# Linear attention and RWKV channel mixing in one kernel: weight halves, new instruction orders and filler matmuls at the start

## Chip, cores and metric

The kernel runs on one core of a Trainium2 chip. The metric is the device time of one execution in microseconds (us); the median of several runs counts. Engines are PE (TensorE), DVE (VectorE), ACT (ScalarE), POOL (GpSimd) and SP (SyncE). PE's matrix results go to PSUM banks, from which DVE or ACT copies them on.

## What is computed

```python
# q, k, v: (8 batches, 8 heads, 576 rows, 64), float32
q_s = softmax(q, axis=-1)                       # over the 64 features of a row
k_s = softmax(k, axis=2)                        # over the 576 rows
kv  = einsum('bhsd,bhse->bhde', k_s, v)
x   = einsum('bhsd,bhde->bhse', q_s, kv)        # heads side by side: (8, 576, 512)

x_prev = x shifted down by one row, first row zero
xk = mu_k * x + (1 - mu_k) * x_prev
xr = mu_r * x + (1 - mu_r) * x_prev
k  = relu(xk @ w_k)                             # (512 x 1024)
v  = (k * k) @ w_v                              # (1024 x 512)
out = sigmoid(xr @ w_r) * v                     # w_r (512 x 512); out (8, 576, 512)
```

## The kernel before

**Attention.** Work comes in units (b, g): batch b and half g of its heads, four heads in two pairs. For each unit ACT takes the exponential of q and k (`exp`) and casts v (`cast_v`), DVE sums q's exponentials (`rsum`), inverts (`rrec`) and scales (`scale_q`, into tiles `qs`). PE transposes the scaled q (`transpose_q`, L498, 36 small matmuls of 64x64 against an identity) and forms kv (`kv`, L475, 36 small matmuls); a column of ones in v's tiles gives the sums for k's softmax. ACT or DVE copies the transposed q to `qt`. For batches 0 and 1 (`ON_PE`) the mixing with `x_prev` is done on PE: DVE makes weights `wp` from kv, its reciprocal sums `rz` and the mu values (`weights_of`, L555), one set for xk and one for xr, and PE multiplies them with `qt` (`by_heads`, L511) for each half h of the 576 rows; ACT or DVE then copies the result into `xk` or `xr` (`copy_mixed`, L568). For the later batches PE only forms x, and DVE does the mixing (L613 to L627).

**Channel mixing.** The rows of four batches lie in a ring of 2304 columns, cut into units of 512, 512, 512, 512 and 256 columns, twice. For each unit PE makes the eight chunks fc of `xk @ w_k` (`k_part`, L712, four matmuls for each chunk over the contraction tiles ct), ACT takes the relu (L697), DVE squares it into `k_a` or `k_b` (L701). Then for every 128 rows PE does `xr @ w_r` (`r_part`, L745), ACT the tanh that makes the sigmoid (L750), PE `k*k @ w_v` in two halves of four matmuls (`v_part`, L755), DVE the gating (L761), and SP stores the rows (L772). In the first two units the chunks are done four at a time, contraction tiles 0 and 1 of all four first (they need only g = 0 and the first half of w_k, `wk0`), then tiles 2 and 3 (g = 1 and `wk1`). These are called the first and the second pairs below; each pair is two matmuls.

**Loads.** The six loads of batch 0 are issued by ACT and SP, in two halves each. All others are issued by POOL and turn float32 weights into bfloat16 on the way; the first of them waits until load number `GATE` of batch 0 has landed. `LOADS` gives their order up to batch 1: `wk0` and `wk1` for w_k, `wv0` and `wv1`, `wr`, `mu`, and names like `q10b` for q of batch 1, group 0, second half. A unit's loads go to buffers `raw_a` to `raw_l`.

**Order.** Nothing is scheduled by hand. Each operation is added to a `Plan` with its engine, an assumed time on the engine and until its result, a key (a due time) and the operations that it depends on. `Plan.order` walks through an assumed time line: on each engine it takes, of the operations that can start within `LOOK` of the earliest, the one that is due first, and it hands out the PSUM slots (`mm_a` to `mm_d`, two `att` slots of two banks) as they come free. The operations are then issued in the order of these starts; the engines run them in that order. Constants of the model (`SPARE`, `LOOK`, `EARLY`, `MAIN`, `PACE`, the DMA terms) therefore decide the order of instructions on every engine, and the chip decides when they run. `ALONE` decides for which units of the later batches the x matmuls are issued alone instead of together with the next unit's transposes.

`filler` emits matmuls of the identity with itself into a free `mm` slot. They have the latest due time, so the planner takes one only when PE has nothing else, and drops those that would start after `FILL_END`:

```python
            if op.due >= 1.5 * LATE and t > FILL_END:
                continue
```

In the kernel before, `FILL` is 0, so there are none.

Of the kernel before, what the change touches and what calls it, by code (L numbers as in the profile page):

```python
# [8 lines left out]
ACT = mybir.ActivationFunctionType  # L9
# [7 lines left out]
START = 0.7  # L17
HOP = 0.05
LATE = 1e6
SPARE = 0.142  # L20
LOOK = {"PE": 0.017, "ACT": 0.686, "DVE": 0.274, "POOL": 0.03, "SP": 0.03}
EARLY = (-0.88, 2.53, 7.27, 7.81, 6.48, 1.05, 4.91, 4.86, 2.31, 3.67, 7.48, 5.23, -5.83,
         4.63, 1.92, 1.86)
EARLY_R = -0.92
MAIN = 17.0
PACE = 1.05
DMA_RATE = 404.0
DMA_LEAD = 1.75
DMA_TAIL = 0.55
# [2 lines left out]
FIRST = ((0, 0, ("ACT", "ACT")), (0, 1, ("SP", "SP")), (0, 2, ("SP", "SP")),  # L32
         (1, 0, ("SP", "SP")), (1, 1, ("SP", "SP")), (1, 2, ("SP", "SP")))
ORDER = (0, 1, 2)
LOADS = ("wk0", "q10b", "wk1", "v10a", "q10a", "wr", "k10a", "wv0", "mu", "v10b", "k10b",
         "wv1", "k11b", "q11b", "q11a", "k11a", "v11a", "v11b")
GATE = 7
FILL = 0
FILL_AT = 1
FILL_END = 15.0  # L40
ON_PE = (0, 1)
CASTS = (("POOL", "POOL"), ("ACT", "DVE"), ("ACT", "ACT"))
QCOPY = ("ACT", "ACT", "DVE")
WIDE = "ACT"
ALONE = 8
EVAC = ((("ACT", "DVE"), ("ACT", "DVE")), (("DVE", "ACT"), ("ACT", "ACT")))


# [23 lines left out]
class Plan:  # L72
# [60 lines left out]
    def order(self):  # L133
        self.set_due()
        free = {}
        self.pe_busy = []
        dma_free = 0.0
        tiled = False
        missing, since = {}, {}
        open_ops = {}  # L140
        for op in self.ops:
            missing[op] = len(op.deps)
            since[op] = 0.0
            open_ops.setdefault(op.engine, [])
            if not op.deps:
                open_ops[op.engine].append(op)
        done = []
        left = len(self.ops)
        while left:
            chosen = None  # L150
            for engine, ops in open_ops.items():
                now = free.get(engine, START)
                ready = None
                for op in ops:
                    t = max(now, since[op])
                    if ready is not None and max(t, now + LOOK[engine]) > ready[0][0]:
                        continue
                    but = []
                    for slot in op.takes:
                        got = self.slot_time(slot, but)  # L160
                        if got is None:
                            break
                        but.append((slot.pool, got[1]))
                        t = max(t, got[0] + HOP)
                    if len(but) < len(op.takes):
                        continue
                    rank = (max(t, now + LOOK[engine]), op.due)
                    if ready is None or rank < ready[0]:
                        ready = (rank, t, op)
                if ready is not None and (chosen is None or ready[1] < chosen[1]):  # L170
                    chosen = ready
            assert chosen is not None, "no operation can start"
            _, t, op = chosen
            open_ops[op.engine].remove(op)
            left -= 1
            if op.due >= 1.5 * LATE and t > FILL_END:
                continue
            for slot in op.takes:
                slot.index = self.slot_time(slot)[1]
                for part in self.pools[slot.pool][slot.index]:  # L180
                    self.user[part] = slot
            occ, lat = op.occ, op.lat
            if op.engine == "PE":
                if not self.warm(t):
                    occ, lat = op.cold * occ, lat + (op.cold - 1) * occ
                if op.tiled != tiled:
                    tiled = op.tiled
                    occ, lat = occ + 0.1, lat + 0.1
                self.pe_busy.append((t, t + occ))
            op.start, op.end = t, t + lat  # L190
            if op.size and op.size < 20:
                op.end += 2.2 if op.key < 0 else 6.0
            elif op.size:
                dma_free = max(dma_free, t + DMA_LEAD) + op.size / DMA_RATE
                op.end = dma_free + DMA_TAIL
                if op.engine == "POOL":
                    op.end += 1.4 if op.size > 1000 else 0.6
            free[op.engine] = t + occ
            for o in self.after.get(op, ()):
                missing[o] -= 1  # L200
                since[o] = max(since[o], op.end + HOP)
                if not missing[o]:
                    open_ops[o.engine].append(o)
            done.append(op)
        return sorted(done, key=lambda o: o.start)
# [3 lines left out]
def kernel(  # L209
# [12 lines left out]
    nc = tc.nc  # L222

    B, H, S, D = q.shape
    C = H * D
    F = moe_w_k.shape[1]
# [3 lines left out]
    FT = F // 128  # L230
# [10 lines left out]
    plan = Plan(pools, shared)  # L241
# [30 lines left out]
    def bank(slot):  # L272
        return ps[slot.pool][slot.index][:]
# [7 lines left out]
    wk_bf = const.tile([128, CT, F], BF16, name="wk_bf")  # L281
# [3 lines left out]
    mu = const.tile([128, 8], F32, name="mu")  # L285
    ident = const.tile([128, 128], BF16, name="ident")
# [64 lines left out]
    mu_slot, rows_slot = Slot("mm"), Slot("mm")  # L351
# [26 lines left out]
    wide = plan.add(WIDE, 0.48 if WIDE == "ACT" else 0.6, 0.6 if WIDE == "ACT" else 0.7, 0, emit_mu_wide, [rows_done], [], [rows_slot])  # L378
    mu_split = [plan.add("POOL", 0.5, 0.6, -2 + m, lambda m=m: emit_mu_rest(m), [wide])
                for m in range(2)]  # L380

    def filler(slot):
        for _ in range(2):
            nc.tensor.matmul(bank(slot)[:, 0:128], lhsT=ident[:], rhs=ident[:], start=True,
                             stop=True)

    gate = [first[GATE]]
    sync = mybir.DependencyInfo(mybir.DependencyClass.Sync, mybir.DependencyReason.DATA)

    def emit_wk(g):  # L390
        ap = bass.AP(tensor=moe_w_k.tensor, offset=moe_w_k.offset + g * 128 * F,
                     ap=[[F, 128], [256 * F, 2], [1, F]])
        return nc.gpsimd.dma_start(out=wk_bf[:, 2 * g:2 * g + 2, :], in_=ap)

    def emit_wr():
        ap = bass.AP(tensor=moe_w_r.tensor, offset=moe_w_r.offset,
                     ap=[[C, 128], [128 * C, CT], [1, C]])
        return nc.gpsimd.dma_start(out=wr_bf[:], in_=ap)

    wk_done, wv_done = [], []  # L400
    for g in range(2):
        wk_done.append(plan.add("POOL", 0.8, 0.8, LOADS.index(f"wk{g}"), lambda g=g: emit_wk(g), gate,
                                size=1140.0))
    wr_done = plan.add("POOL", 0.8, 0.8, LOADS.index("wr"), emit_wr, gate, size=1140.0)
    mu_load = plan.add("POOL", 1.2, 1.2, LOADS.index("mu"), emit_mu_load, gate, size=10.0)
    mu_t = plan.add("PE", 0.2, 0.4, LATE, emit_mu, [mu_load, consts], [mu_slot])
    mu_done = plan.add("DVE", 0.08, 0.17, LATE, emit_mu_copy, [mu_t], gives=[mu_slot])

    def emit_wv(h):
        n = FT // 2  # L410
        ap = bass.AP(tensor=moe_w_v.tensor, offset=moe_w_v.offset + h * n * C,
                     ap=[[FT * C, 128], [C, n], [1, C]])
        return nc.gpsimd.dma_start(out=wv_bf[:, h * n:(h + 1) * n, :], in_=ap)

    for h in range(2):
        wv_done.append(plan.add("POOL", 0.8, 0.8, LOADS.index(f"wv{h}"), lambda h=h: emit_wv(h), gate,
                                size=1140.0))
    for b in range(1, B):
        for g in range(2):
            for n, i in enumerate(ORDER):  # L420
# [9 lines left out]
    warmed = []  # L430
# [244 lines left out]

    for _ in range(FILL):
        slot = Slot("mm")
        plan.add("PE", 0.12, 0.25, 2 * LATE, lambda slot=slot: filler(slot), [warmed[0]], [slot],
                 [slot])


# [3 lines left out]
    def unit(half, c0, n):  # L685
# [24 lines left out]
        def k_part(kf, fc, cts):  # L710
            for ct in cts:
                nc.tensor.matmul(bank(kf)[:, 0:n],  # L712
                                 lhsT=wk_bf[:, ct, fc::FT],
                                 rhs=xs[0][:, ct, c0:c0 + n],
                                 start=(ct == 0), stop=(ct == CT - 1))

# [133 lines left out]
```

## Time and profile before

| | |
|---|---|
| median of 7 runs | 203.37 us (202.43 to 203.87) |
| profiled execution, its own time | 203.84 us |
| its span, first to last instruction | 202.1 us |
| PE busy | 186.9 us, 2171 matmuls |
| weight loads on PE | 104.2 us (beside the matmuls) |
| DVE busy | 162.7 us, 348 instructions |
| ACT busy | 137.2 us, 212 instructions |
| POOL busy | 40.5 us |
| HBM | 33.56 MB read, 9.44 MB written |

The profile comes from one execution. Busy time of PE is modelled: matmuls overlap, so the busy time of single ones adds up to more than the time that they take in a row. A view called the chain of waits follows the work that ended last back from the end, at each step to what released it. A view by stretches gives the busy time of each engine in a window of the span, and a view of waits says what each engine waited for. Line numbers are those of the kernel before; in the changed kernel the same lines stand 6 further down from L445 on (L712 becomes L718, for example).

### The profile page before, as it was taken

What the parts mean: (1) busy time and instruction counts of PE and PEld (TensorE: products, weight loads), DVE (VectorE), ACT (ScalarE), POOL (GpSimd) and SP (SyncE); (2) the same over time, 40 slices, a digit from 0 to 9 for tenths busy, and PEclk for the clock granted to TensorE, in tenths of its full rate; (3) what the DMA queues carried; (4) which work ended last, traced back from release to release, by engine and by line L of the source; (5) the groups of instructions that cost most, each with busy time, mean ns of one, the idle gap of its engine ahead of it and who ended that gap; (6) DMA issues with size and microseconds to landing.
All of it is one profiled execution on the core that took longest, in us unless ns stands there. A gap on an engine that the chain in (4) does not pass through costs nothing.

```text
span 202.1 us, 5333 instructions
## 1 busy us (share of the span) xinstructions
PE 186.9 (92%) x2171; PEld 104.2 (52%) x2171; DVE 162.7 (81%) x348; ACT 137.2 (68%) x212; POOL 40.5 (20%) x65
## 2 busy tenths in 40 slices
PE   2358999899999999999999999999999999999992
PEld 0144454356444663564576565456456544654761
DVE  2698573897999999999989999999999879732531
ACT  4693589589899789968499777945744653552440
POOL 1592466643143312411140000000000000000000
PEclk9999999999999999999999999999999999999999
DMA  6999999999999988994897040242025113402524
GB/s 199 358 256 271 247 290 404 390 400 407 391 402 403 401 343 242 274 343 177 256 292 249 13 97 3 52 107 54 3 54 125 34 33 74 104 0 52 115 44 104
DMA packets 15248, 40.72 MB, mean 202 GB/s; under 512 B 2284, under 2 KB 3064, under 8 KB 15224
## 3 DMA queue, kind: packets, MB, share of 16 engines
q0 software_dynamic: 7568, 27.40, 41.1%
q1 hardware_dynamic: 7208, 12.26, 20.9%
q10 hardware_dynamic: 448, 0.72, 1.3%
q8 instruction: 17, 0.28, 0.6%
q14 instruction: 7, 0.06, 0.1%
HBM read 33.56 MB, written 9.44 MB: 213 GB/s over the span
## 4 chain that ended last, share of the span: by engine, by line
PE 86%; DVE 6%; DMA 4%; ACT 1%; issue 0%; DVEq 0%; ACTq 0%
PE mm_b L755 10%; PE mm_d L712 9%; PE mm_c L712 8%; PE mm_c L755 7%; PE mm_a L755 7%; PE mm_d L755 7%; PE mm_b L712 7%; PE mm_a L712 5%; PE mm_c L745 4%; PE mm_a L745 4%; PE mm_d L745 3%; PE mm_b L745 3%; PE att_b L511 3%; DMA raw_d<-in_q_dram 3%; PE att_a L511 3%; PE att_b L498 2%
## 5 line engine op out<-in xcount | busy, mean ns | idle before, releaser
L712 PEld LDWEIGHTS <-wk_bf 128*128 128x128 bf16 x320 | 43.6, 145 | 21.0 <-issue 2.4
L712 PE MATMUL mm_d<-xk,wk_bf 128*128 128x512 bf16 (+1 forms) x96 | 24.5, 368 | 0.0
L755 PEld LDWEIGHTS <-k_b 128*128 128x128 bf16 x152 | 14.3, 98 | 15.3 <-issue 0.5
L745 PEld LDWEIGHTS <-xr 128*128 128x128 bf16 x144 | 13.9, 98 | 15.9 <-issue 0.2
L755 PEld LDWEIGHTS <-k_a 128*128 128x128 bf16 x144 | 13.4, 98 | 15.7 <-issue 0.9
L712 PE MATMUL mm_c<-xk,wk_bf 128*128 128x512 bf16 (+1 forms) x84 | 20.9, 362 | 0.0
L712 PE MATMUL mm_b<-xk,wk_bf 128*128 128x512 bf16 (+1 forms) x76 | 19.4, 370 | 0.0
L712 PE MATMUL mm_a<-xk,wk_bf 128*128 128x512 bf16 (+1 forms) x64 | 15.6, 361 | 0.0
L755 PE MATMUL mm_b<-wv_bf,k_b 128*128 128x512 bf16 (+1 forms) x56 | 13.5, 364 | 0.0
L745 PE MATMUL mm_c<-wr_bf,xr 128*128 128x512 bf16 x44 | 11.3, 379 | 0.0
L755 PE MATMUL mm_c<-wv_bf,k_a 128*128 128x512 bf16 x40 | 10.3, 380 | 0.0
L755 PE MATMUL mm_b<-wv_bf,k_a 128*128 128x512 bf16 x40 | 10.3, 380 | 0.0
L745 PE MATMUL mm_a<-wr_bf,xr 128*128 128x512 bf16 x40 | 10.3, 379 | 0.0
L755 PE MATMUL mm_a<-wv_bf,k_b 128*128 128x512 bf16 x32 | 8.2, 380 | 0.0
L755 PE MATMUL mm_a<-wv_bf,k_a 128*128 128x512 bf16 x32 | 8.2, 380 | 0.0
L755 PE MATMUL mm_d<-wv_bf,k_a 128*128 128x512 bf16 x32 | 8.2, 380 | 0.0
L745 PE MATMUL mm_d<-wr_bf,xr 128*128 128x512 bf16 x32 | 8.2, 379 | 0.0
L755 PE MATMUL mm_d<-wv_bf,k_b 128*128 128x512 bf16 x32 | 8.2, 379 | 0.0
L750 ACT ACTIVATE th_a<-mm_c 128x512 f32<-128x512 f32 x10 | 6.0, 603 | 3.1 <-PE mm_c L745 3.1
L755 PE MATMUL mm_c<-wv_bf,k_b 128*128 128x512 bf16 (+1 forms) x32 | 7.4, 353 | 0.0
L750 ACT ACTIVATE th_b<-mm_a 128x512 f32<-128x512 f32 x7 | 4.2, 602 | 4.5 <-PE mm_a L745 2.3
L745 PE MATMUL mm_b<-wr_bf,xr 128*128 128x512 bf16 x28 | 7.2, 379 | 0.0
(268 smaller groups left out, 416.4 us busy)
## 6 DMA issues: line engine op xcount, KB each, us to landing
out_dram<-ot_a SPq DMA_DIRECT2D x24, 128.0 KB, 4.8
out_dram<-ot_b SPq DMA_DIRECT2D x24, 128.0 KB, 3.7
out_dram<-ot_c SPq DMA_DIRECT2D x22, 128.0 KB, 2.4
raw_a<-in_q_dram POOLq DMA_DIRECT2D x3, 576.0 KB, 7.9
raw_c<-in_v_dram POOLq DMA_DIRECT2D x3, 576.0 KB, 7.9
raw_b<-in_k_dram POOLq DMA_DIRECT2D x2, 576.0 KB, 10.3
raw_d<-in_q_dram POOLq DMA_DIRECT2D x2, 576.0 KB, 10.5
raw_e<-in_k_dram POOLq DMA_DIRECT2D x2, 576.0 KB, 8.8
```

Of the source, the lines that this page charges most:

```text
L498: nc.tensor.transpose(out=transposed()[64 * u:64 * u + 64, hf, 64 * j:64 * j + 64], in_=qss[qs.index][r, j, 64 * u:64 * u + 64], identity= ...
L511: nc.tensor.matmul(bank(xp)[64 * hf:64 * hf + 64, u, at + c:at + e], lhsT=w[r, hf, :], rhs=qts[qt.index][r, hf, src:src + e - c], start=(n ...
L712: nc.tensor.matmul(bank(kf)[:, 0:n], lhsT=wk_bf[:, ct, fc::FT], rhs=xs[0][:, ct, c0:c0 + n], start=(ct == 0), stop=(ct == CT - 1))
L745: nc.tensor.matmul(bank(rps), lhsT=xs[1][:, ct, c:c + 128], rhs=wr_bf[:, ct // 2 + 2 * (ct % 2), :], start=(ct == 0), stop=(ct == CT - 1))
L750: nc.scalar.activation(out=ths[th.index][:], in_=bank(rps), func=ACT.Tanh, scale=0.5)
L755: nc.tensor.matmul(bank(vps)[:, 0:w], lhsT=k2s[k2.index][:, ft, 128 * m:128 * m + 128], rhs=wv_bf[:, ft, e:e + w], start=(ft == 0), stop=( ...
```

## The change

It does several things at once. The first half of w_k (`wk0`) is loaded in two column halves, `wk0a` and `wk0b`; `wk1` stays whole. For this the chunks take columns 4 apart from one column half (0 to 511 or 512 to 1023) instead of columns 8 apart from all 1024, and the two halves of w_v become contiguous blocks to match. The order of loads is another one, with `q10a` first. Up to 60 fillers are planned, from the kv matmuls of unit (0, 0) to 16 us on the planner's time line; each is one matmul of 256 columns. The planner's constants differ, among them the assumed sizes and tails of the DMAs, and with them the order of instructions on PE, ACT, DVE and POOL.

```diff
-SPARE = 0.142
-LOOK = {"PE": 0.017, "ACT": 0.686, "DVE": 0.274, "POOL": 0.03, "SP": 0.03}
-EARLY = (-0.88, 2.53, 7.27, 7.81, 6.48, 1.05, 4.91, 4.86, 2.31, 3.67, 7.48, 5.23, -5.83,
-         4.63, 1.92, 1.86)
-EARLY_R = -0.92
-MAIN = 17.0
-PACE = 1.05
+SPARE = 0.367
+LOOK = {"PE": 0.014, "ACT": 0.49, "DVE": 0.274, "POOL": 0.03, "SP": 0.03}
+EARLY = (-4.56, 2.11, 8.25, 13.06, 6.4, 0.7, -0.55, -0.78, 2.62, 0.78, 6.17, 8.08, -3.7,
+         4.17, 15.59, 5.15)
+EARLY_R = 3.13
+MAIN = 14.0
+PACE = 1.2
...
-LOADS = ("wk0", "q10b", "wk1", "v10a", "q10a", "wr", "k10a", "wv0", "mu", "v10b", "k10b",
-         "wv1", "k11b", "q11b", "q11a", "k11a", "v11a", "v11b")
+LOADS = ("q10a", "wk0a", "wk0b", "wk1", "k10a", "q10b", "wr", "mu", "v10b", "v10a", "k10b",
+         "wv0", "q11b", "wv1", "q11a", "k11b", "k11a", "v11a", "v11b")
 GATE = 7
-FILL = 0
+FILL = 60
 FILL_AT = 1
-FILL_END = 15.0
+FILL_END = 16.0
...
-ALONE = 8
+ALONE = 6
...
                 if op.engine == "POOL":
-                    op.end += 1.4 if op.size > 1000 else 0.6
+                    op.end += 1.0 if op.size > 600 else 0.8
...
     def filler(slot):
-        for _ in range(2):
-            nc.tensor.matmul(bank(slot)[:, 0:128], lhsT=ident[:], rhs=ident[:], start=True,
-                             stop=True)
+        nc.tensor.matmul(bank(slot)[:, 0:256], lhsT=ident[:],
+                         rhs=ident[:, None, :].to_broadcast((128, 2, 128)), start=True, stop=True)
...
-    def emit_wk(g):
-        ap = bass.AP(tensor=moe_w_k.tensor, offset=moe_w_k.offset + g * 128 * F,
-                     ap=[[F, 128], [256 * F, 2], [1, F]])
-        return nc.gpsimd.dma_start(out=wk_bf[:, 2 * g:2 * g + 2, :], in_=ap)
+    def emit_wk(g, c, e):
+        ap = bass.AP(tensor=moe_w_k.tensor, offset=moe_w_k.offset + g * 128 * F + c,
+                     ap=[[F, 128], [256 * F, 2], [1, e - c]])
+        return nc.gpsimd.dma_start(out=wk_bf[:, 2 * g:2 * g + 2, c:e], in_=ap)
...
-        wk_done.append(plan.add("POOL", 0.8, 0.8, LOADS.index(f"wk{g}"), lambda g=g: emit_wk(g), gate,
-                                size=1140.0))
+    for name in LOADS:
+        if name.startswith("wk"):
+            g = int(name[2])
+            c, e = {"": (0, F), "a": (0, F // 2), "b": (F // 2, F)}[name[3:]]
+            o = plan.add("POOL", 0.8, 0.8, LOADS.index(name),
+                         lambda g=g, c=c, e=e: emit_wk(g, c, e), gate, size=1250.0 * (e - c) / F)
+            for h in range(2):
+                if c <= h * F // 2 < e:
+                    wk_done[g, h] = o
...
     def emit_wv(h):
         n = FT // 2
-        ap = bass.AP(tensor=moe_w_v.tensor, offset=moe_w_v.offset + h * n * C,
-                     ap=[[FT * C, 128], [C, n], [1, C]])
+        ap = bass.AP(tensor=moe_w_v.tensor, offset=moe_w_v.offset + h * n * 128 * C,
+                     ap=[[n * C, 128], [C, n], [1, C]])
...
-                                 lhsT=wk_bf[:, ct, fc::FT],
+                                 lhsT=wk_bf[:, ct, F // 2 * (fc // 4) + fc % 4:F // 2 * (fc // 4 + 1):4],
...
-                        + [wk_done[h] for h in gs] + [mms_[i]],
+                        + [wk_done[h, fc // 4] for h in gs] + [mms_[i]],
```

More of the change, by code (lines that the diff above doesn't have):

```diff
@@ L377 @@
     rows_done = plan.add("PE", 0.86, 0.98, -501, emit_mu_rows, [rows_load, consts], [rows_slot])
-    wide = plan.add(WIDE, 0.48 if WIDE == "ACT" else 0.6, 0.6 if WIDE == "ACT" else 0.7, 0, emit_mu_wide, [rows_done], [], [rows_slot])
+    wide = plan.add(WIDE, *{"ACT": (0.48, 0.6), "DVE": (0.6, 0.7), "POOL": (0.75, 0.85)}[WIDE], 0,
+                    emit_mu_wide, [rows_done], [], [rows_slot])
     mu_split = [plan.add("POOL", 0.5, 0.6, -2 + m, lambda m=m: emit_mu_rest(m), [wide])
@@ L398, in emit_wr @@
         return nc.gpsimd.dma_start(out=wr_bf[:], in_=ap)
-    wk_done, wv_done = [], []
-    for g in range(2):
-        wk_done.append(plan.add("POOL", 0.8, 0.8, LOADS.index(f"wk{g}"), lambda g=g: emit_wk(g), gate,
-                                size=1140.0))
-    wr_done = plan.add("POOL", 0.8, 0.8, LOADS.index("wr"), emit_wr, gate, size=1140.0)
+    wk_done, wv_done = {}, []
+    for name in LOADS:
[7 more added lines that the diff above has]
+                    wk_done[g, h] = o
+    wr_done = plan.add("POOL", 0.8, 0.8, LOADS.index("wr"), emit_wr, gate, size=1200.0)
     mu_load = plan.add("POOL", 1.2, 1.2, LOADS.index("mu"), emit_mu_load, gate, size=10.0)
@@ L416 @@
         wv_done.append(plan.add("POOL", 0.8, 0.8, LOADS.index(f"wv{h}"), lambda h=h: emit_wv(h), gate,
-                                size=1140.0))
+                                size=1200.0))
     for b in range(1, B):
@@ L677 @@
         slot = Slot("mm")
-        plan.add("PE", 0.12, 0.25, 2 * LATE, lambda slot=slot: filler(slot), [warmed[0]], [slot],
+        plan.add("PE", 0.108, 0.25, 2 * LATE, lambda slot=slot: filler(slot), [warmed[0]], [slot],
                  [slot])
```

## The prediction

> **What bounds it now.** First the head of the page.
>
> ```profile
> span 202.1 us, 5333 instructions
> PE 186.9 (92%) x2171; PEld 104.2 (52%) x2171; DVE 162.7 (81%) x348; ACT 137.2 (68%) x212; POOL 40.5 (20%) x65
> PEclk9999999999999999999999999999999999999999
> PE 86%; DVE 6%; DMA 4%; ACT 1%; issue 0%; DVEq 0%; ACTq 0%
> ```
>
> PE carries the chain that ended last. Where it does not, the view by stretches shows (columns: busy us of PE, weight loads, DVE, ACT, POOL with instruction counts, clock, DMA share, GB/s):
>
> ```profile
> 10.45:13.06 2.61, 0.34 (x7) 0.13 (x2) 2.61 (x7) 2.42 (x5) 2.61 (x5) 1.00 1.02 279
> 60.00:150.00 90.00, 89.91 (x1105) 50.45 (x1103) 87.11 (x178) 71.00 (x106) 12.39 (x18) 1.00 0.59 191
> ```
>
> From 10.45 to 13.06 PE is almost idle. From 60 to 150 it never is, but DVE works 87 of those 90 us too: two engines share the bound there. Then the chain between 9 and 24 us, in order of time (start, us, what):
>
> ```profile
> 9.92 1.51 DVE rsum_b L458 x2
> ...
> 11.68 1.34 DVE qs_b L466 x2
> 13.02 0.04 issue
> 13.06 0.69 PE att_b L498 x20
> ...
> 15.75 0.65 ACT xk L568
> ...
> 17.61 1.00 PE mm_c L712 x2
> 18.61 0.85 PE mm_d L712 x2
> 19.47 0.85 PE mm_a L712 x2
> 20.32 0.85 PE mm_b L712 x2
> ...
> 23.10 0.59 PE mm_c L712 x2
> 23.69 0.43 PE mm_d L712 x2
> ```
>
> This is the place that matters. The same instruction pair (two 128x512 matmuls) takes 0.85 us until 21.2 and 0.43 us from 23.1: PE runs at half speed until about 22 us. PEclk does not show it (a 9 in every slice); the trace's clock record agrees with the chain, it only begins at 22.3 us. After 23.1 PE waits once for long, in the view of waits:
>
> ```profile
> PE att_b L498 <- ACT xr L568: 0.7, 1, 0.7
> ```
>
> That is 39.77 to 40.48, before the transposes of batch 1, group 1. So all there is to win lies before 23.1 (half speed) and in this 0.7 us. Everything after is a string of matmuls at 0.216 us that no order can shorten.
>
> **The change, part by part.**
>
> *Fillers.* 60 are asked for; the built program keeps 24, the planner drops the rest. On PE: kv(0,0), 12 fillers, transposes(0,1), 8 fillers, mixing, 3, mixing, 1, then the first L718 pair. At half speed one filler (256 columns) takes half a 512-column matmul, 0.43/2 = 0.21 us. ACT now makes the mu copy after one half of ek_a rather than before it, so POOL's mu_rest and its v cast come some 0.3 us later, and kv(0,0) ends at 10.8 instead of 10.45. Twelve fillers then end at 10.8 + 2.56 = 13.4, against 13.06 for the transposes: 0.3 us late. This costs nothing by itself, since ACT is busy with qt_a until 13.8 before it takes qt_b. The eight behind the transposes cost 1.7 us at half speed, 0.9 at full; there PE would wait for wp_a (ready at 14.4), so their overhang is 0.6 to 1.4 us and lies on the path.
>
> *When full speed comes.* Before, 3.6 us of dense L712 matmuls (17.54 to 21.1) were followed by full speed at 22.3. Counted over all PE work almost without a pause, it took 5.9 us (from 16.44). With dense work from 10.8 on, that puts full speed between 10.8 + 3.6 = 14.4 and 10.8 + 5.9 = 16.7; I take the middle, 15.5.
>
> The Trainium skill ("TensorE: Matmul & The Clock Gate", "What's actually happening") says that the gate looks at free-running windows of 3.4 us, so the moment shifts from run to run; no single trace shows that. Its Part 4 says that transposes do not count as busy, which speaks against the 36 transposes between the two groups of fillers: by that the late bound would hold, and the sum below would be 0.5 us higher.
>
> *Up to the second L718 pairs (before: 23.10).* With full speed at 15.5, from the built order and the durations of before's rows: mixing(0,0) half 1 at 15.65 to 15.95, DVE copies it until 16.7; then rz_b 0.2, wp_c 0.5, rsum_c 0.7, rrec_c 0.2 and the copy of x(0,1) 0.7, which reaches 19.0; wp_d 0.55, qs_a 0.7 and the xr copy 0.7 reach 20.9; the last mixing 0.37 ends at 21.3. On PE four L718 pairs at 0.43 and the mixing fit between these. So the second pairs start at 21.3, where DVE is what they wait for: **1.8 us earlier**. With full speed at 14.4 the eight fillers and the mixing behind them end 0.4 us sooner and the second pairs start at 20.9; at 16.7 they end 0.5 us later, at 21.8 (2.2 and 1.3 us).
>
> *Loads.* The floor under this is the load of wk1, which the second pairs read. wk0 landed at 16.4 (issued 10.23, 6.2 us), wk1 at 20.0 (11.68, 8.3 us). One 288 KB half of q sits before wk1 in both orders, so the same bytes precede it: 20.0 again, not the last to arrive. The column halves need some 0.7 us more of issue on POOL (one issue took 0.72 to 0.89), whose queue runs ahead of the transfers anyway, and their 512 KB follow 288 KB loads that landed 0.7 us apart (410 GB/s), so no loss of rate: 0 (bounds -0.3 to +0.5). wk0a lands about 15.7, before anything wants it. Later landings, each moved by the bytes before it: k10b 26.1 (was 29.0), wv0 28.5 (27.0), wv1 31.6 (31.4), v11b 35.8 (the same). On ACT the v casts and ek_a of batch 1 now stand before the relu of chunks 5 to 7, so PE's L751 for mm_d waits until k10b is in: 26.1 plus one exp and one relu behind the casts, 28.1. PE gets there at 28.0 to 28.4. It is nearly a tie; any more lateness of that load is paid one for one.
>
> *Order up to 41 us.* Transposes and kv(1,0) move from 32.4 to about 28, ahead of two r groups, and the halves of q(1,1) are summed and scaled one by one on DVE. Then transposes(1,1) no longer wait for both: the stall of **0.7 us** goes. Next late there is v11b (cast done about 36.7), and PE comes at 38: covered by 1.3 us.
>
> *From 41 us on.* PE has the same matmuls and, counting both built orders, the same cost of switching between attention and matmul work (177.4 us either way, without fillers). I summed the rows' durations on DVE that stand ahead of each PE instruction that needs DVE, and the PE work ahead of it. Before, the margin is smallest around L511 at 123 us (+0.2 us, and PE waited 0.25 there). In the new order the margin is -0.03 to +0.02 at three places between about 120 and 132 us and +0.3 at 150. So PE meets DVE more often: I take **0.5 us** lost, bounds 0 (PE meets it nowhere) and 1.9 (DVE keeps none of the lead beyond what it had in before).
>
> *Smaller parts.* wk's column step falls from 8 to 4 elements: its weight loads take 145 ns against 98 for k_b, but a group of four L712 matmuls takes 0.86 us like one of L745, so they are hidden; 0, at most 0.06 us on some 15 groups that follow a switch. The wv halves become contiguous, their packets keep 8 KB: 0. ALONE joins two more blocks, already in the 177.4.
>
> *Sum*, against the profiled execution: 203.84 (202.1 span and 1.7 around it) - 1.8 - 0.7 + 0.5 = **201.8**. That execution is 0.5 above the median of 203.37, and near the top of seven (202.43 to 203.87); a half-speed phase that ends at a varying moment would spread them so, and I make no correction.
>
> **Rivals.**
> 1. *Given back to DVE* (20%). The 87.11 of 90 us speak for it: if DVE cannot start its long run earlier, PE catches up and the full 1.9 us is lost: 203.2. Against: DVE's run began after a wait of 3.1 us for kv(1,0), which now comes 4 us earlier.
> 2. *The fillers do not raise the clock* (14%; slower). Place: the pairs from the second L718 group on. The fillers' overhang of 1.4 us stays, the four pairs run at 0.85, the second group starts at 22.2 (0.9 earlier), and then about 3.4 us of dense work must run at half speed before the clock rises, losing 1.7: 203.84 - 0.9 + 1.7 - 0.7 = 203.9 if the later PE no longer meets DVE, 204.4 if it still loses 0.5 there. It decides if those pairs take 0.85 us. For it: 17.5 to 21.1 was dense and still slow. Against: the fillers give more than five dense us before 16.
> 3. *The loads decide* (6%). If k10b lands 3 us late, at 29.0 as before, ACT holds three relus and PE stands some 2.5 us: 204.3.
>
> **How the numbers follow.** My forecast, 60%: 200.6 to 202.3 (full speed at 14.4, no loss to DVE and 0.3 from the loads; full speed at 16.7 with the loss of 0.5). Rival 1 fills 202.3 to 203.7, rivals 2 and 3 reach 204.4. A range of 200.6 to 203.7 leaves out under 2 in 10. Measurement tells about 0.3% from no change, so the borders are 202.76 and 203.98. Faster: 0.60 and a third of rival 1, 0.66. Same: the rest of rival 1 and a little of rival 2, 0.17. Slower: most of 2, all of 3, 0.17.
>
> **What would show it.** Right: the clock record begins near 15 us; L718 pairs take 0.43 from the first; the second group starts at 21.3; no PE wait before transposes(1,1); PE's waits for DVE after 100 us sum to under 1 us. Wrong: first pairs at 0.85 (rival 2); PE standing at 28 us behind ek_a (rival 3); L517 waiting for DVE's w between 100 and 150 us by more than 1 us (rival 1).

## The result: 205.15 us, 0.85% slower, and the profile after

The changed kernel takes 205.15 us (median of 15 runs, 203.68 to 207.58) against 203.37 us; the ratio is 1.0085, with a 95% interval of 1.0065 to 1.0105. The forecast was 201.8. Medians here and below are of all executions of a run; ratios leave out those that took over 1.5% longer than the fastest of their kernel. The profiled execution took 205.56 us. The line numbers in the fences below are those of the changed kernel.

The head of the page, which answers to the first fence of the prediction:

```profile
span 203.6 us, 5385 instructions
...
PE 188.2 (92%) x2195; PEld 97.9 (48%) x2195; DVE 161.3 (79%) x348; ACT 137.0 (67%) x212; POOL 40.9 (20%) x66
```

DVE and the weight loads do less than before, PE has 24 matmuls more. In the view by stretches PE, which was idle for 0.1 us between 60 and 150 us in before, now is for 3.2 us:

```profile
60.00:150.00 90.00, 86.81 (x1084) 45.50 (x1083) 84.21 (x174) 70.88 (x103) 11.37 (x16) 1.00 0.59 195
```

The next fence is the chain of waits (start, us, what), first at the beginning, where the prediction expected its gain:

```profile
3.86 6.92 DMA raw_d<-in_q_dram
...
12.52 6.29 DMA wk_bf<-in_moe_w_k_dram
...
18.85 0.41 PE mm_c L718
19.26 0.40 PE att_b L517 x8
...
19.75 0.76 DVE xk L574
...
22.85 0.56 PE mm_c L718 x2
23.41 0.43 PE mm_d L718 x2
```

The first L718 pair begins at 17.88, and its second matmul stands until a load of w_k lands at 18.80. All that follows on DVE stands behind that, and the second pairs come at 22.85: not at 21.3 as forecast, hardly before the 23.10 of the kernel before. Then the chain between 75 and 79 us:

```profile
75.37 0.32 PE att_b L504 x36
75.69 0.26 PE att_b L481 x31
75.95 2.27 issue
78.22 0.24 PE att_b L481 x5
78.46 0.97 PE mm_d L761 x4
```

PE does 31 of the 36 kv matmuls, stands for 2.27 us, and does the other five. The profile shows nothing that it waits for ("issue"). Such a pause is called a stand below. The view of what PE waited for has both losses:

```profile
PE att_b L481 <- issue: 2.3, 1, 2.3
PE mm_c L718 <- DMA wk_bf<-in_moe_w_k_dram: 0.6, 1, 0.6
PE mm_c L481 <- POOL vv_a L457: 0.5, 2, 0.3
PE mm_c L718 <- issue: 0.5, 1, 0.5
```

The last line is a second stand, of 0.52 us, at 109.6 us. The wait for ACT's xr, 0.7 us in before, is no longer there.

### The profile page after: what moved, and what is told of

Its sections match the earlier page's. It is cut to its first block, busy times and chain, and to the rows that moved or that the text cites. A ratio compares the mean times of both kernels' runs of the same rounds, so it can differ in the third digit from the quotient of the medians.

```text
span 203.6 us, 5385 instructions
## 1 busy us (share of the span) xinstructions
PE 188.2 (92%) x2195; PEld 97.9 (48%) x2195; DVE 161.3 (79%) x348; ACT 137.0 (67%) x212; POOL 40.9 (20%) x66
## 4 chain that ended last, share of the span: by engine, by line
PE 85%; DMA 8%; DVE 3%; issue 2%; POOL 1%; SPq 0%; ACT 0%; DVEq 0%
PE mm_c L761 10%; PE mm_a L718 9%; PE mm_d L718 8%; PE mm_d L761 8%; PE mm_a L761 6%; PE mm_c L718 6%; PE mm_b L761 6%; PE mm_b L718 6%; PE mm_b L751 6%; PE mm_d L751 4%; DMA raw_d<-in_q_dram 3%; DMA wk_bf<-in_moe_w_k_dram 3%; PE mm_c L751 3%; PE mm_a L751 3%; PE att_a L517 2%; PE att_b L517 2%
## 5 line engine op out<-in xcount | busy, mean ns | idle before, releaser
L718 PEld LDWEIGHTS <-wk_bf 128*128 128x128 bf16 x320 | 35.2, 114 | 28.3 <-issue 1.5
L718 PE MATMUL mm_a<-xk,wk_bf 128*128 128x512 bf16 (+1 forms) x100 | 24.5, 359 | 0.0
L761 PEld LDWEIGHTS <-k_b 128*128 128x128 bf16 x152 | 14.5, 98 | 15.7 <-issue 0.7
L718 PE MATMUL mm_d<-xk,wk_bf 128*128 128x512 bf16 (+1 forms) x88 | 22.0, 365 | 0.0
L751 PEld LDWEIGHTS <-xr 128*128 128x128 bf16 x144 | 13.9, 98 | 15.9
L718 PE MATMUL mm_c<-xk,wk_bf 128*128 128x512 bf16 (+1 forms) x68 | 16.5, 356 | 1.1 <-DMA wk_bf<-in_moe_w_k_dram 0.6
L718 PE MATMUL mm_b<-xk,wk_bf 128*128 128x512 bf16 (+1 forms) x64 | 15.6, 353 | 0.0
L751 PE MATMUL mm_b<-wr_bf,xr 128*128 128x512 bf16 x52 | 13.4, 379 | 0.0
L761 PE MATMUL mm_c<-wv_bf,k_b 128*128 128x512 bf16 x48 | 12.3, 379 | 0.0
L756 ACT ACTIVATE th_a<-mm_b 128x512 f32<-128x512 f32 x12 | 7.1, 595 | 6.4 <-PE mm_b L751 4.9
L761 PE MATMUL mm_a<-wv_bf,k_b 128*128 128x512 bf16 (+1 forms) x40 | 9.4, 358 | 0.0
L707 DVE TENSOR_TENSOR k_a<-rel_b 128x512 bf16<-128x512 bf16 (+1 forms) x14 | 5.6, 397 | 3.4 <-ACT rel_b L703 3.3
L707 DVE TENSOR_TENSOR k_a<-rel_c 128x512 bf16<-128x512 bf16 (+1 forms) x13 | 5.0, 388 | 3.4 <-ACT rel_c L703 3.4
L751 PE MATMUL mm_c<-wr_bf,xr 128*128 128x512 bf16 x28 | 7.2, 379 | 0.0
```

The source lines that it names most:

```text
L707: nc.vector.tensor_tensor(out=k2s[k2.index][:, fc, 0:n], in0=rels[rel.index][:, 0:n], in1=rels[rel.index][:, 0:n], op=ALU.mult)
L718: nc.tensor.matmul(bank(kf)[:, 0:n], lhsT=wk_bf[:, ct, F // 2 * (fc // 4) + fc % 4:F // 2 * (fc // 4 + 1):4], rhs=xs[0][:, ct, c0:c0 + n], ...
L751: nc.tensor.matmul(bank(rps), lhsT=xs[1][:, ct, c:c + 128], rhs=wr_bf[:, ct // 2 + 2 * (ct % 2), :], start=(ct == 0), stop=(ct == CT - 1))
L756: nc.scalar.activation(out=ths[th.index][:], in_=bank(rps), func=ACT.Tanh, scale=0.5)
L761: nc.tensor.matmul(bank(vps)[:, 0:w], lhsT=k2s[k2.index][:, ft, 128 * m:128 * m + 128], rhs=wv_bf[:, ft, e:e + w], start=(ft == 0), stop=( ...
```

## The experiments

The theories were: A, PE stands because its next instructions have not been fetched yet; B, the stand is an accident of traffic or belongs to the kv matmuls themselves; C, the matmuls on `wk0a` wait for `wk0b`; D, the fillers bring nothing and cost nothing; E, more work ahead or a longer program removes the stand by itself. Two came later: F, POOL's late issue of k10b takes back what the fillers win; G, the fillers' gain is lost elsewhere or is not there.

### First series: the same again, three tiles, no fillers

Both kernels were run once more unchanged, with a profile each (one execution each).

> The changed kernel once more, unchanged, for one more profile. Theory A (the lost time is a stall of PE for its own code: a 16 KB instruction fetch that falls into the kv block near 76 us): PE stands again about 2.3 us at the same instruction of that block, and nothing is waited for. Rival B (the stall is an accident of DMA traffic in one execution): it is gone or stands elsewhere by more than 50 instructions. Theory C (the first L718 pair is held by wk0b): the second matmul of the first pair again begins with wk0b's landing near 18.8 us.

Measured: 206.49 us. The same 31 matmuls, then a stand at 76.30; wk0b's landing at 19.16 again ends a wait in the first pair:

```profile
PE att_b L481 <- issue: 2.2, 1, 2.2
...
PE mm_c L718 <- DMA wk_bf<-in_moe_w_k_dram: 1.4, 1, 1.4
```

Both stands are back at the same instructions, so they are no accident (B in its first form falls).

> The kernel before once more, unchanged, for one more profile. If the 0.86 us by which batch 0's loads landed later in the profile of the changed kernel is a spread from run to run, raw_d lands anywhere from 9.9 to 10.8 us here; if the change makes it, it lands near 9.9 again. Theory A expects no stall of PE without a wait over 1 us before 100 us, since the fetch near 74 us falls among long matmuls here.

Measured: 203.35 us. No stand without a wait over 0.3 us before 100 us. raw_d (q of batch 0, group 1) landed at 10.55 with its second half, against 9.93 in the first profile of before and 10.79 and 10.99 in those of the changed kernel. So this is a spread from run to run: over all profiles of this study it lands between 9.5 and 11.7 us, though the loads of batch 0 are the same. What sets it stayed open; it moves the start of single executions by more than several of the effects looked for here.

The next kernel, sep, has three tiles in place of one for w_k:

```diff
-    wk_bf = const.tile([128, CT, F], BF16, name="wk_bf")
+    wk_0a = const.tile([128, 2, F // 2], BF16, name="wk_0a")
+    wk_0b = const.tile([128, 2, F // 2], BF16, name="wk_0b")
+    wk_1 = const.tile([128, 2, F], BF16, name="wk_1")
```

> The changed kernel with wk0a, wk0b and wk1 in three tiles of their own; same order, same number of instructions. Theory C (the matmuls on wk0a wait for wk0b because both lie in one tile in crossing address spans): the first L718 pair no longer waits for the second load, begins near 17.0 us, the second pairs come about 0.9 us earlier than 22.85, and the time falls by 0.5 to 1.0 us to about 204.4. Theory A: the stall near 76 us stays, since the code is the same length. Rival (the second pairs are held by DVE or by wk1's landing anyway): no change, within 0.2 us.

Measured: 205.54 us, ratio 1.0089 (1.0057 to 1.0121): no gain in the median, where theory C expected 0.5 to 1.0 us. In the chain of its profile (raw_d landed at 9.46) the first pair waits for nothing, and the second pairs (L720 here) begin with wk1:

```profile
11.90 8.94 DMA wk<-in_moe_w_k_dram
20.84 0.05 issue
20.89 0.62 PE mm_c L720 x2
```

From raw_d's landing to the second pairs that is 11.4 us, against 12.1 and 12.2 in the two profiles with one tile. So theory C is right about the wait, worth some 0.7 us in these profiles. Why the median does not fall stayed open. The executions go by their clock: six of twelve have a mean clock of 0.989 to 0.992 and take 205.8 to 206.6 us, the other six 0.997 to 1.0 and 203.7 to 205.3. But the changed kernel has as many at a low clock, eight of sixteen at 0.992 or less, so the clock does not set the two apart; among the executions above 0.992 the median is 204.7 us here and 205.0 there. The stand stays, 2.33 us at 74.09, as theory A expected.

Then the changed kernel without its fillers (nofill):

```diff
     def filler(slot):
-        nc.tensor.matmul(bank(slot)[:, 0:256], lhsT=ident[:],
-                         rhs=ident[:, None, :].to_broadcast((128, 2, 128)), start=True, stop=True)
+        return None
```

> The changed kernel without its 24 filler matmuls, all else in the same order; PE has 48 instructions less. Theory A: the fetch boundary moves 48 instructions on, out of the kv block into longer matmuls, and the stall of 2.3 us near 76 us goes; without the fillers full speed comes only near 21 us, which costs 1 to 2 us at the start: between 203.5 and 205.2 us in all. Rival D (the fillers themselves bring nothing at the start and cost nothing): same time, 205.2. Rival B (stall by traffic, not position): the stall stays and the time rises to 206 to 207 us.

Measured: 203.57 us, ratio 0.9983 (0.9953 to 1.0013), 1% better than with fillers; no stand without a wait. A fits (it expected 203.5 to 205.2), D falls.

### Second series: moving the code, not the work

Here PE's instructions are counted from the first in the trace, as number 0: weight loads, matmuls and the few semaphore and drain records between them. Beside them stand the packets of 16,384 bytes of the DMA queue that brings instructions: 17 in these programs, 17 or 18 in those below.

```
kernel        PE stands at      previous border   code packet   PE goes on   packet to
              instruction       passed at (us)    starts        at           going on
changed       1985              72.61             75.87         78.22        2.35
changed       2753             104.85            107.72        110.08        2.36
changed again 1985              72.96             76.03         78.53        2.50
three tiles   1985              70.75             73.89         76.42        2.53
before        (1985, no stand)  73.41             74.30         -            -
```

1985 and 2753 are 193 and 7 or 10 times 256. In every program there are as many such places, from 193 on, as packets: PE's code comes in blocks of 256 instructions, and these places are called borders here. Between the borders 1729 and 1985 most of the instructions belong to two attention groups of 144 tiny ones, which PE runs in 0.6 to 0.7 us each, so it is through the block 3.3 us after the border, and only then, 3.3 us after the border too, does the packet with the next block start. In before the border 1985 is crossed 6.6 us after 1729, among long matmuls. The 24 fillers are 48 instructions; with the new order they decide where the borders fall.

All 18 profiles of this study agree. In each of them the first packet is taken to bring the code behind the second border, the second packet that behind the third, and so on. Of 296 borders PE passes none less than 2.2 us after its packet has started. Ten are passed 2.2 to 2.55 us after it, and nine of these are the nine stands; the other 286 are passed 2.6 us after it or later, none with a stand.

The page "Runtime: NRT & Kernel Launch" of the Trainium skill (section "Instruction fetch mechanics") says that code is refilled in blocks of 16 KiB, 256 instructions, which these numbers show, and that crossing a border is mostly hidden, which at these two places it is not.

This is still an agreement of times. The test moves the borders and leaves the work in place: it puts small matmuls of the identity ahead of the first matmul, where PE waits 3.8 us for mu_rows. There are 104 of them here, 128 and 52 in the kernels after it:

```diff
     def emit_mu_rows():
+        for _ in range(104):
+            nc.tensor.matmul(bank(rows_slot)[0:64, 0:64], lhsT=ident[0:64, 0:64],
+                             rhs=ident[0:64, 0:64], start=True, stop=True)
```

> The changed kernel with 104 matmuls of 64x64 of the identity put ahead of the L365 matmul, where PE waits 3.8 us for mu_rows: 208 PE instructions more, some 2 us of work in that wait; all else the same. Theory A (blocks of 256 PE instructions; PE stands when two block borders follow within about 5.5 us): the borders move 208 instructions forward to places 6 us or more apart, no stall near 76 or 109 us, and the time falls by the 2.3 us and some 0.5: 202.0 to 203.0 us, below before. Rival B (the stall belongs to the kv matmuls themselves, their data or the DMA traffic there): it stays, 205.2 us or a little more.

Measured: 203.34 us, ratio 0.9982 (0.9961 to 1.0004). No stand anywhere after the start. So B falls too. Theory A's number was 202.0 to 203.0: the small matmuls took until 7.1 us (the expectation of pad88 below says 6.4), longer than the 2 us thought, and delayed the start.

> As pad104, but 128 small matmuls: 256 PE instructions more, one whole block. Theory A: all borders fall where they fell without them, one block number higher; the stall of 2.2 to 2.5 us at the same matmul of the kv block is back, 205 to 206 us. Rival E (more work ahead or a longer program removes the stall by itself): no stall, the time of pad104.

Measured: 208.52 us, ratio 1.0232 (1.018 to 1.0284). The stand is back after the same 31 matmuls, at instruction 2241 (1985 and 256), and again at 3009. Its chain and, below, the view by stretches (columns as in the prediction):

```profile
78.34 0.26 PE att_b L484 x31
78.60 2.50 issue
81.10 0.25 PE att_b L484 x5
81.35 0.97 PE mm_d L764 x4
82.31 1.48 PE mm_a L754 x4
83.80 1.71 PE mm_b L754 x4
85.50 1.09 PE mm_c L764 x4
```

```profile
76.00:78.00 2.00, 2.00 (x36) 0.89 (x38) 2.00 (x8) 2.00 (x3) 0.94 (x2) 1.00 0.99 394
78.40:81.20 2.80, 0.30 (x30) 0.19 (x16) 2.06 (x3) 1.03 (x2) 0.79 (x2) 1.00 0.98 355
82.30:85.80 3.50, 3.50 (x11) 1.20 (x9) 1.71 (x5) 1.27 (x3) 0.72 (x1) 0.52 0.98 340
85.80:90.00 4.20, 4.20 (x96) 2.21 (x95) 3.33 (x8) 4.07 (x7) 1.09 (x2) 1.00 0.67 177
```

More work and a longer program do not cure it; one whole block brings it back (E falls). And it shows what a stand can cost besides: four L754 matmuls take 1.71 instead of 0.86 us, and the granted clock is 0.52 between 82.3 and 85.8. The clock record has half speed from 82.42 to 85.83, one window of 3.41 us, right behind the window in which PE stood for 2.1 us. This adds some 1.7 us (and the 128 small matmuls cost 2.65 at the start). One window of half speed in some 190 us lowers the mean clock by 0.009, to 0.99. In the kernels whose profiles have stands 18 of 37 executions have a mean clock of 0.992 or less, in all the others of the study 9 of 110. So a stand probably costs 2.3 us in some executions and 4 in others. That is not shown directly: pad128's is the only profile with such a window behind a stand, and a window of half speed also comes without one (pad104's profile has it from 21.4 us on, behind the wait for wk0b).

> pad104 with wk0a, wk0b and wk1 in three tiles as in sep. Theory A and C: no stall, and no wait of the first L718 pair for wk0b: 0.5 to 1.0 us below pad104, 201.2 to 202.4 us, the fastest so far. Rival (the wait for wk0b is hidden by DVE or by wk1): equal to pad104 within 0.3 us.

Measured: 203.23 us, ratio 0.9966 (0.9948 to 0.9984); all twelve executions have a clock of 0.996 or more. That is only 0.1 us below pad104's median, where theory C expected 0.5 to 1.0, though the highest of twelve is 203.9, not 204.7.

> The kernel before with 52 small matmuls ahead of L365: 104 PE instructions more, in the wait for mu_rows. Counted over the trace of before, that puts two borders into the kv and transpose blocks near 74 us, 1.1 us apart, and others near 107 and 124 us. Theory A: PE stands about 4 us near 74 us and 0.5 to 1.6 us at each of the others; the time rises by 3 to 6.5 us to 206.5 to 210 us. Rival B or E: 203.4 us as before.

Measured: 206.89 us, ratio 1.0161 (1.0116 to 1.0206). The kernel before, with nothing changed in its own work, loses 3.0 us:

```profile
74.57 0.33 PE att_a L501 x36
74.89 0.19 PE att_a L478 x23
75.08 2.20 issue
77.29 0.31 PE att_a L478 x13
```

The border is 1985 again, the packet starts at 74.97, PE goes on 2.31 later. Followed matmul by matmul, the kernel is 0.8 us late from the start, by the time of the small matmuls, and 3.2 us after this place. Of the three stands foretold only this one came, and 2.2 us long where 4 were expected: the blocks whose packets start at 107.88 and 124.63 were there in time, though PE needed them 4.8 and 3.9 us after the border before. All nine stands lie where it would have needed them within 5 us, so that close spacing is needed for a stand and not enough for one. The time from a border to the start of the next packet was 1.2 to 3.5 us before the stands; what sets it stayed open.

### Third series: what is left without the stands

The small matmuls are made 32x32 with 16 columns, 88 of them (176 instructions); they end before mu_rows is there, and the first matmul of the kernel begins at 3.80 us as without them.

> The changed kernel with 88 small matmuls of the identity (32x32 weights, 16 columns) ahead of L365: 176 PE instructions more. In pad104 the small matmuls took until 6.4 us and pushed L365's matmul back by 2.5 us; these are a quarter of the size and should end before 5 us. Theory A: no stall for code anywhere, and no half-speed window behind one; 202.5 to 203.3 us, at or up to 0.8 below pad104. Rival B: 205 us.

Measured: 203.12 us, ratio 0.9979 (0.9951 to 1.0008). Against the profile of the changed kernel, each matmul comes 0.24 us later between 20 and 72 us, 2.22 earlier from 82, and 2.62 earlier from 128 on. These are 2.86 us in all, and the two stands took 2.27 and 0.52.

> pad88 with wk0a, wk0b and wk1 in three tiles. Theory C: first L718 pair without the wait for wk0b, the second pairs begin with wk1's landing; 0.5 to 1.0 us below pad88, 201.6 to 202.6 us. Rival: within 0.2 us of pad88, since wk1's landing or DVE sets the start of the second pairs in most executions.

Measured: 202.68 us, ratio 0.996 (0.993 to 0.9989): 0.4 us below pad88, just under what theory C expected (0.5 to 1.0), and with overlapping intervals. Its second pairs begin at 21.43, but then PE waits, which no earlier profile showed:

```profile
PE att_a L486 <- ACT ek_a L456: 0.5, 1, 0.5
```

ACT has waited for the second half of k of batch 1 (k10b), landed at 28.4.

The next kernel, whole_pad88, is pad88 with the first half of w_k in one load again:

```diff
     def emit_wk(g, c, e):
+        if c:
+            return None
         ap = bass.AP(tensor=moe_w_k.tensor, offset=moe_w_k.offset + g * 128 * F,
-                     ap=[[F, 128], [256 * F, 2], [1, e - c]])
+                     ap=[[F, 128], [256 * F, 2], [1, F]])
```

> pad88 with the first half of w_k loaded by one DMA of 512 KB, issued where wk0a is issued. If the column halves only bring a wait (theory C), the first L718 pair waits until this one landing (about 0.5 us before that of wk0b, since one issue of 0.7 us less stands on POOL) and the time is that of pad88 or up to 0.5 below. Rival (the halves pay, as the change means them to): 0.3 to 1 us above pad88.

Measured: 202.62 us, ratio 0.9929 (0.9894 to 0.9964), 0.5% below pad88 with overlapping intervals: no sign that the halves pay. The profiles show what the halves do to the loads. One load of 512 KB was in 5.1 to 7.0 us after its issue in six profiles (5.1 in this one); both halves were in 6.3 to 8.2 us after the issue of wk0a in twelve. The loads behind come later too. Counted from raw_d's landing, wk1 lands after 9.1 to 10.5 us with one load and 10.5 to 11.7 with halves, and k10b after 15.9 to 16.8 us in the three kernels with one load in this order and 17.4 to 17.9 in nine profiles with halves (those with 104 and 128 small matmuls, whose loads start later, are left out). In the traces the halves are 512 packets of 1,024 bytes, the one load 256 of 2,048. That this makes the difference was not tested.

> sep without the 24 fillers (its borders fall as in nofill, so no stall for code). Against sep_pad88 this is the worth of the fillers alone. If they earn what the prediction says, 1.3 to 2.2 us above sep_pad88; if the second pairs wait for wk1 or DVE anyway, 0 to 0.7 us above it.

Measured: 202.01 us, ratio 0.9922 (0.9894 to 0.9949), and not above sep_pad88 but below it, with overlapping intervals. So the fillers earn nothing that the median shows, even where they cost no stand.

### Fourth series: where the fillers' gain goes

The view of POOL's issues of sep_pad88 (start, us, what, and in brackets the idle time before and what ended it):

```profile
17.08 0.58 POOL L310 DMA_DIRECT2D raw_i<-in_v_dram  x1 [0.31 <-DMA wk_0a<-in_moe_w_k_dram]
...
19.19 0.55 POOL L310 DMA_DIRECT2D raw_i<-in_v_dram  x1 [1.53 <-DMA wk_0b<-in_moe_w_k_dram]
...
21.67 0.54 POOL L310 DMA_DIRECT2D raw_h<-in_k_dram  x1 [1.93 <-DMA wk<-in_moe_w_k_dram]
```

POOL does not run ahead of the transfers freely: each of these issues begins when the load eight issues before has landed. The trace of the changed kernel has the reason. Its loads on POOL take eight semaphores in turn (111 to 118), and each issue from the ninth on waits for its own, so this is a wait in the program. k10b (the last line) goes out only when wk1 is in. Two tiny loads of mu were moved behind it:

```diff
-LOADS = ("q10a", "wk0a", "wk0b", "wk1", "k10a", "q10b", "wr", "mu", "v10b", "v10a", "k10b",
-         "wv0", "q11b", "wv1", "q11a", "k11b", "k11a", "v11a", "v11b")
+LOADS = ("q10a", "wk0a", "wk0b", "wk1", "k10a", "q10b", "wr", "v10b", "v10a", "k10b", "mu",
+         "wv0", "q11b", "wv1", "q11a", "k11b", "k11a", "v11a", "v11b")
```

> sep_pad88 with the two loads of mu (2 KB each, needed late) issued behind k10b; the order on PE, DVE and ACT is the same. In sep_pad88 POOL issued k10b only at 21.67 us, when wk1 had landed eight issues earlier, and kv(1,0) waited 0.5 us for it near 29 us. Theory F (POOL's issues wait for the landing of the load eight issues before, and k10b takes back what the fillers win): k10b is issued near 17 us, the wait of kv(1,0) goes, the time falls by 0.3 to 0.7 us to 202.0 to 202.4. Rival G (the gain of the fillers is lost elsewhere or is not there): 202.7 as sep_pad88.

Measured: 202.25 us, ratio 0.9921 (0.9889 to 0.9952). k10b was issued at 17.46 and still landed at 28.84, and ACT waited for it (ACT's instructions in order of time):

```profile
28.86 0.68 ACT L456 ACTIVATE ek_a<-raw_h 128x576 bf16<-128x576 f32 x1 [0.76 <-DMA raw_h<-in_k_dram]
```

An issue 4.2 us earlier brought no earlier landing (17.7 us after raw_d in both profiles), so the late issue is not what holds it. The time is 0.4 us lower, with overlapping intervals, and by this profile not for the reason that F gave.

> sep_nofill with the mu loads behind k10b. Without fillers PE reaches kv(1,0) about 0.8 us later, and k10b was there in time. Theory F: no change against sep_nofill, 202.0, and now 0.3 to 1.0 above sep_pad88_mu. Rival G: within 0.3 us of sep_pad88_mu or below it.

Measured: 201.86 us, ratio 0.9917 (0.9897 to 0.9937), the lowest median of the study, 1.7 us (0.8%) below before and 1.7% below the changed kernel by their ratios.

> whole_pad88 (the first half of w_k in one load, fillers, 88 small matmuls) with the mu loads behind k10b. One issue less stands ahead of k10b. Theory F: within 0.2 of sep_pad88_mu or up to 0.5 below it (201.5 to 202.3). If separate column halves pay: 0.3 to 1 above it.

Measured: 203.38 us, ratio 0.994 (0.9906 to 0.9975), outside what either side expected. raw_d landed at 11.7 in its profile, the latest of all, and single executions lay between 200.95 and 205.22.

> The same without fillers and without the small matmuls: from the change only the orders, the load order and the new column grouping are left. Theory F: 0.3 to 1.0 us above whole_pad88_mu. Rival G: equal to it within 0.3 us or below; then what is won over the kernel before comes from the orders alone.

Measured: 202.16 us, ratio 0.9917 (0.9893 to 0.9942). So in three pairs without a stand in either, the kernel without fillers is 0.4% (sep), 0.04% (sep, mu late) and 0.2% (whole, mu late) below the one with them, and in the fourth (nofill and pad88) 0.04% above it, all with overlapping intervals. F falls as it was put: an earlier issue of k10b does not bring the gain back, and no median shows one. The profiles show where it is lost, though. At equal amounts of PE's work sep_pad88 is 0.8 us ahead of sep_nofill at 28 us and 0.1 ahead at 30, and sep_pad88_mu is 0.6 ahead of sep_nofill_mu at 28 and 0.3 behind at 30. Between lies PE's wait for ek_a behind k10b's landing, 0.5 and 0.7 us long. What is left in whole_nofill_mu, the orders (mu late) and the new column grouping alone, is worth 0.8%.

## Why the prediction was wrong, step by step

**The sum lacked a term.** It counted the fillers' time and not their number; of the rest it said that PE has "the same matmuls" and "a string of matmuls at 0.216 us that no order can shorten". 48 instructions more, in a new order, put two code borders where PE needs its next block within 5 us. That is 2.27 and 0.52 us in the profile, and probably 1.7 more in executions in which a half-speed window follows. From the changed kernel (1.0085) to pad88 (0.9979) it is 1.06%, some 2.1 us: more than the whole loss. None of the rivals had it. The trace of before held the rows, unread: the code packets, and that of 74.3 us, which started some 120 instructions later in its block than most, between tiny matmuls.

The two profiled executions add up so, compared at equal amounts of PE's work (output columns). The changed kernel is 0.3 us ahead of before at 30 us, where 1.8 were forecast; it gains 1.1 more until 46 us, where 0.7 were forecast; then it loses 3.0, where 0.5 were forecast, and 2.8 of these are the two stands. That is 1.6 us behind, and 0.2 more lie outside the span: 1.7 in all.

**"The column halves ... 0 (bounds -0.3 to +0.5)" and "wk0a lands about 15.7, before anything wants it".** Wrong. wk0a landed at 16.67, and PE could not use it alone: a wk0b that takes columns 512 to 1023 of two contraction tiles spans, in one tile's flat addresses, columns 0 to 511 of the second, and the automatic waits go by the span: the weight load of ct 1 in the first pair waits for wk0b's semaphore, and three tiles take that wait away. PE's waits in the first pair were 0.6 to 1.7 us in the profiles with halves in one tile, with mixing of the other half queued behind the waiting weight load, which the prediction did not ask. Worth in the median: 0.2% (pad88 to sep_pad88), within the noise.

**"Up to the second L718 pairs ... 1.8 us earlier".** Mechanism half right, worth wrong. Full clock came at 15.60 us, forecast 15.5, bounds 14.4 to 16.7; L718 pairs take 0.43 us. That it came so near is luck: the same kernel got it at 13.19 in its other profile. The late bound of 16.7, which the prediction also drew from the transposes, held in neither. In ten further profiles with fillers it came between 12.4 and 18.7, in the ones without between 17.2 and 22.5. But the second pairs hardly came earlier: counted from raw_d's landing, 12.1 and 12.2 us in the two profiles of the changed kernel, 13.2 and 12.2 in those of before. With three tiles it is 10.6 to 11.4 us in the four profiles with fillers and 11.8 to 11.9 in the two without: the fillers do win 0.4 to 1.3 us there, and in the two pairs of profiles above it is lost near 29 us, behind k10b. The step that failed beside the wait for wk0b is the floor of the loads, "whose queue runs ahead of the transfers anyway, and their 512 KB follow 288 KB loads ...: no loss of rate". POOL's issues wait for the landing eight issues before, and with the halves the loads behind land later: wk1 at 21.30 in the changed kernel's profile (forecast 20.0), k10b at 28.58 (forecast 26.1; counted from raw_d 17.8 us, forecast 16.2). Rival 3 (the loads decide) had 6% and is the nearest to this part, but PE did not wait for k10b in the changed kernel. That k10b is all that eats the fillers' gain was not tested, since it was not made to land earlier in a kernel with halves.

**"The stall of 0.7 us goes".** Right. Compared at equal amounts of PE's work, sep_nofill gains 1.0 us on before between 30 and 46 us and keeps it.

**"0.5 us lost to DVE from 41 us on".** Within its bounds, at their lower end. Without the stands PE's stream is rigid after 30 us: between kernels of this order the distance changes at one place, near 105 us, and by no more than 0.5 us. Rival 1 (given back to DVE) falls. The weight loads' 145 ns became 114 and, hidden, moved nothing. The packets of the wv loads have 4,096 bytes in the traces of both kernels, not the 8 KB of the prediction, and moved nothing either. Rival 2 (the clock does not rise) falls with the 15.60.

## What to carry to other kernels

An instruction that costs no time still takes a place in the code. Where a stream of long matmuls holds groups of a hundred and more tiny ones, count the instructions from border to border (256 here), and test a change of their number with a harmless pad before its work is blamed. When a load is split so that its first part can be used sooner, give each part its own tile, or see that its flat span does not cover what the other part's readers want, and look at what the split does to the loads behind it.

## What was not expected of the hardware

- A PE that runs out of code goes on 2.2 to 2.5 us after its 16,384-byte packet starts, in the nine stands measured. 104 instructions put ahead of the kernel before cost it 1.6%, three quarters of it by one stand.
- The clock record has whole windows: 53, 55 or 56 times 3.413 us in the profiles of before and after. A PE idle for 2.1 us of one such window (pad128), and for about 1.7 of one (pad104, at the start), got half speed for the next; with 1.5, 1.7 and 1.9 us (sep, after_again, before_pad52) it did not, so the idle time in a window does not decide alone. The Trainium skill ("TensorE: Matmul & The Clock Gate", "What's actually happening") gives the window as 3413 ns, free-running, which agrees. In "Why this matters for your kernels" it speaks of gaps over some 3 us for a fall back to half speed; the gaps here were 2.5 us (pad128) and 1.7 us (pad104).
- Issuing a load 4.2 us sooner did not make it land sooner (k10b, sep_pad88 and sep_pad88_mu).
